# Attention outputs turned by VectorE in 32-squares and divided by their row sums only after the gather

## The chip, the cores and the metric

The kernel runs on one core of one Trainium2 chip. The metric is the device time of the whole program in microseconds (us), as the median of several executions. A core has five engines that run side by side, each through its own list of instructions in order, and that wait for one another by semaphores: TensorE (PE in the profile; PEld is its loading of weights), VectorE (DVE), ScalarE (ACT), GpSimd (POOL) and SyncE (SP, which here only issues transfers). Sixteen DMA engines move data between the chip's main memory (DRAM) and the on-chip memory; matrix products land in a second on-chip memory (PSUM)[...].

## The reference: attention with a threshold, then a layer of experts chosen by hash

```python
def _attn_ref(q, k, v, tau):                       # (8, 8, 576, 64): batch, heads, seq, head_dim
    scale = 1.0 / np.sqrt(q.shape[-1])
    scores = scale * np.matmul(q, k.transpose(0, 1, 3, 2))
    thresh = np.max(scores, axis=-1, keepdims=True) - tau
    scores = np.where(scores >= thresh, scores, -1000000000.0)
    scores = scores - np.max(scores, axis=-1, keepdims=True)
    attn = np.exp(scores)
    attn = attn / (np.sum(attn, axis=-1, keepdims=True) + 1e-09)
    return np.matmul(attn, v)
# the bridge: x[b * 576 + s, 64 * h + d], that is (4608, 512)
def _moe_ref(x, token_ids, w1, w2):                # 8 experts, w1 (8, 512, 1024), w2 (8, 1024, 512)
    expert_idx = token_ids * np.int64(2654435761) % np.int64(8)
    for e in range(8):
        mask = expert_idx == e
        out[mask] = np.maximum(x[mask] @ w1[e], 0.0) @ w2[e]
```

Everything is in 32-bit floats. The division by the row sum can be done before or after the product with v, and also after x has been written to DRAM and gathered again, since one row of x has one sum per head.

## The kernel before

The attention works on 32 pairs of heads (8 batches by 4 pairs; `p` counts pairs, `hp` is the place of the pair among four). A pair has five steps (`s`, or `n` counted over all pairs): step 0 holds the 64 last queries of both heads, steps 1 to 4 hold 128 queries of each head. Per step and head, TensorE makes scores (`score`), VectorE negates them, takes the extreme of each row and moves them out of PSUM (`negate`), ScalarE takes the exponential (`expo`), and VectorE applies the threshold and sums the rows (`mask`). Two steps later TensorE turns the weights (`turn_w`), ScalarE moves them out (`put_wT`), and TensorE multiplies by v (`av_part`), which leaves the output of a pair as 128 rows (head, d) by 576 columns (queries). That output has to be turned, divided and written to the scratch `x_dram`, one row per token:

```python
x_dram = nc.dram_tensor("x_scratch", (N, DIN), FP32, kind="Internal").ap()
x_rows = x_dram.rearrange("n (h d) -> (n h) d", h=HP)
...
def scale_k(p):
    nc.gpsimd.tensor_scalar(out=kts[p][:], in0=kts[p][:], scalar1=keep_any[:],
                            scalar2=SCALE, op0=ALU.mult, op1=ALU.mult)
...
def turn(dst, src, cols):                   # 64x64 transposes on TensorE, two row halves at a time
    for c, (lo, hi) in enumerate(cols):
        for r, c0 in ((0, lo), (1, hi)):
            rows = slice(64 * r, 64 * r + 64)
            nc.tensor.transpose(dst[:, r, 64 * c:64 * c + 64], src[rows, c0:c0 + P],
                                ident[rows, rows])
...
def put_oT(g):                              # PSUM -> SBUF, g = 0: 320 queries, g = 1: 256
    c0, width = ((64, WA), (64 + WA, WB))[g]
    nc.scalar.copy(oT[:, c0:c0 + width], av[:, g, 0:width])

def turn_o():
    turn(av, oT, [(P * (t + 1), P * (t + 1)) for t in range(NQ)] + [(64, 0)])

def add_eps(p):                             # row sums + 1e-9 into rec, on GpSimd
    ...
def put_xm(p):
    rec = recs.pop(p)
    xm = a_x.tile([P, NS, P], FP32, name="xm")
    nc.vector.tensor_tensor(                # PSUM -> SBUF, times 1 / row sum
        out=xm[:].rearrange("p t (j d) -> p t j d", j=2),
        in0=av[:, :, 0:NS * D].rearrange("p j (t d) -> p t j d", t=NS),
        in1=rec[:]. ... .to_broadcast([P, NS, 2, D]), op=ALU.mult)
    r0, c0 = x_place(p)
    nc.sync.dma_start(out=x_dram[r0:r0 + TAIL, c0:c0 + P].rearrange("(t p) m -> p t m", p=P),
                      in_=xm[:, 0:NQ])
    for j in range(2):
        ...                                 # the 64 tail rows, one transfer for each head
```

The order of one step, cut to what touches this:

```python
for n in range(LAST + NS + 1):
    p, s = divmod(n, NS); m = n - 2; q = p - 1
    ...                                     # loads for pair p + 2
    if s == 1 and 0 <= q < NP:
        add_eps(q)
    if s == 1 and p + 1 < NP:
        scale_k(p + 1)
    if s == 2 and 0 <= q < NP:
        nc.vector.reciprocal(recs[q][:], recs[q][:])
    if s == 0 and p >= 2:
        turn_o()
    ...                                     # av_part, negate, expo, put_oT(0) at s == 2, turn_w, put_wT
    if s == 0 and n < LAST:
        next(pieces, None)                  # a piece of the routing; another at s == 3
    if s == 0 and p >= 2 and n != LAST:
        put_xm(p - 2)
    if s == 4 and 0 <= q < NP:
        put_oT(1)
    ...                                     # turn_w, score(n + 1), put_wT
    if 0 < n <= LAST:
        for j in range(heads(n - 1)):
            mask(n - 1, j)
    ...
```

While the last pairs run, three quarters of the rows of expert 0 are gathered already (`fetch_0`), turned by TensorE (`early_xT`) and multiplied (`early_h`, taken in small portions by `fill`); the last quarter follows after the last pair:

```python
for kt in range(KT):
    fetch_0(kt, HP - 1)
fill(FO * 2 * (CO - 1) - 18)
tr = ps_tr.tile([P, 2, 512], FP32, name="tr")
early_xT(tr, 0, KT, CO - 1, CO)
```

The experts 1 to 7 gather their rows by index (`fetch`), VectorE turns them in 32-squares, and transfers put the squares in place:

```python
def turn_x(e):
    for k in range(KT):                     # KT = 5 blocks of 128 rows
        nc.vector.transpose(out=xq[:, :, 32 * k:32 * k + 32],
                            in_=xg_sets[e % 2][k][:].rearrange("p (d a) -> p d a", a=32))
    for g in range(4):
        ...                                 # xq -> xT, 16 transfers
```

Two products with ReLU between them (`gemm1`, `gemm2`, `gemm2_last`) and the scatter of the results end each expert.

Of the kernel before, what the change touches and what calls it, by code (L numbers as in the profile page):

```python
# [20 lines left out]
def kernel(  # L21
# [12 lines left out]
    nc = tc.nc  # L34
# [37 lines left out]
    x_dram = nc.dram_tensor("x_scratch", (N, DIN), FP32, kind="Internal").ap()  # L72
# [16 lines left out]
    keep_any = consts.tile([P, 1], FP32, name="keep_any")  # L89
# [14 lines left out]
    xg_bufs = [consts.tile([P, DIN], FP32, name=f"xg_{i}") for i in range(KT)]  # L104
# [10 lines left out]
    def fetch_0(kt, hp):  # L115
        gather(x_rows, xg_bufs[kt][:, P * hp:P * hp + P], gidx_0[:, kt, hp:hp + 1])
# [11 lines left out]
    with tc.tile_pool(name="a_q", bufs=1) as a_q, \  # L128
# [25 lines left out]
        oT = a_o.tile([P, 64 + S], FP32, name="oT")  # L154
        av = ps_av.tile([P, 2, 512], FP32, name="av")
        kts, rss, recs, scs, nss, stats, ws = {}, {}, {}, {}, {}, {}, {}

        def load_pair(p):
# [23 lines left out]
            for r in range(2):  # L182
                queries(nc.scalar, r, TAIL, S)
            for c0, c1 in ((0, P), (P, TAIL)):
                for r in range(2):
                    queries(nc.sync, r, c0, c1)
# [11 lines left out]
        def scale_k(p):  # L198
            nc.gpsimd.tensor_scalar(out=kts[p][:], in0=kts[p][:], scalar1=keep_any[:],
                                    scalar2=SCALE, op0=ALU.mult, op1=ALU.mult)  # L200
# [4 lines left out]
        def score(n, j):  # L205
# [8 lines left out]
            for h in range(2) if s == 0 else (j,):  # L214
                out_rows = slice(64 * h, 64 * h + 64) if s == 0 else slice(0, P)
                q0, q1 = (TAIL, S) if s == 0 else (P * (s - 1), P * s)
# [94 lines left out]
        def put_oT(g):  # L311
            c0, width = ((64, WA), (64 + WA, WB))[g]
            nc.scalar.copy(oT[:, c0:c0 + width], av[:, g, 0:width])

        def turn_o():
            turn(av, oT, [(P * (t + 1), P * (t + 1)) for t in range(NQ)] + [(64, 0)])

        def x_place(p):
            hp, b = divmod(p, B)
            return b * S, hp * P  # L320

        def add_eps(p):

            rec = a_st.tile([P, 2 * NS], FP32, name="rec")
            rs = rss.pop(p)
            for i, cols in ((0, 9), (9, 1)):
                nc.gpsimd.tensor_scalar(out=rec[:, i:i + cols], in0=rs[:, i - i // 9:i - i // 9 + cols],
                                        scalar1=1e-9, scalar2=None, op0=ALU.add)
            recs[p] = rec

        def put_xm(p):


            rec = recs.pop(p)
            xm = a_x.tile([P, NS, P], FP32, name="xm")
            nc.vector.tensor_tensor(
                out=xm[:].rearrange("p t (j d) -> p t j d", j=2),
                in0=av[:, :, 0:NS * D].rearrange("p j (t d) -> p t j d", t=NS),
                in1=rec[:].rearrange("p (t j) -> p t j", j=2)[:, :, :, None]
                .to_broadcast([P, NS, 2, D]), op=ALU.mult)  # L340
            r0, c0 = x_place(p)
            nc.sync.dma_start(
                out=x_dram[r0:r0 + TAIL, c0:c0 + P].rearrange("(t p) m -> p t m", p=P),
                in_=xm[:, 0:NQ])
            for j in range(2):
                cols = slice(D * j, D * j + D)
                nc.sync.dma_start(out=x_dram[r0 + TAIL:r0 + S, c0 + D * j:c0 + D * j + D],
                                  in_=xm[64 * j:64 * j + 64, NQ, cols])
# [54 lines left out]

# [117 lines left out]
        make_identity(nc, ident[:])  # L521
# [8 lines left out]
        nc.vector.memset(oT[:, 0:64], 0.0)  # L530
        nc.vector.memset(xg_bufs[0][:], 0.0)
        nc.scalar.activation(none_f[:], none_f[:], AF.Exp)
# [16 lines left out]
        def early_xT(tr, k0, k1, c0, c1):  # L549

            blocks = [(kt, co) for kt in range(k0, k1) for co in range(c0, c1)]
            for i, (kt, co) in enumerate(blocks):
                for r in (0, 64):
                    r1 = min(r + 64, TROWS[kt])
                    nc.tensor.transpose(tr[:, r // 64, 64 * i:64 * i + r1 - r],
                                        xg_bufs[kt][r:r1, P * co:P * co + P],
# [62 lines left out]
        with tc.manual_schedule():  # L619

            tr = ps_tr.tile([P, 2, 512], FP32, name="tr")
            for _ in range(16):
# [324 lines left out]
```

## Time and profile before

| | before |
|---|---|
| time, median of 3 | 1008.86 us (1008.33 to 1008.9) |
| span of the profiled execution | 1001.3 us |
| PE busy | 983.8 us (98%) |
| DVE busy | 517.7 us (52%), nearly all of it in the attention |
| ACT busy | 436.9 us (44%) |
| POOL busy | 291.7 us (29%) |
| DMA | 145779 packets, 117.07 MB; 59860 packets under 512 B |
| attention, about | 0 to 454 us of the span |
| passage to the experts, about | 454 to 498 us |
| experts, about | 498 to 1001 us |

The span is one execution under the profiler, a little shorter than the time that is measured around it; differences of the one are read beside differences of the other. A row of groups gives the line of the kernel, the engine, the operation, what it writes and reads, its shape and count, then the total busy time, the mean duration of one in ns, and the idle time of the engine just before, with what ended it. Instructions of one engine overlap at their ends: the next one starts before the last has been completed. So where an engine is full, the cost of an instruction is the distance from its start to the next one's start, which the timeline shows, and not its duration. Busy shares of PE have to be read with care: matmuls are pipelined, and their ends are modelled.

### The profile page before, as it was taken

To read this page: it belongs to the slowest core of one execution; us is meant where nothing else is said; L and a number is where in the kernel's file an instruction comes from. 1 tells how busy PE (TensorE), PEld (TensorE's weight loads), DVE (VectorE), ACT (ScalarE), POOL (GpSimd) and SP (SyncE) were. 2 spreads that over 40 slices of the span, in tenths; PEclk is the share of its full clock that TensorE was granted. 3 is DMA by queue.
4 is the path that set the end of the run, shared out by engine and by line. 5 is a ranking of instruction groups with operands and counts; after the bars stand their busy time and mean duration, and the time that the engine had idled before them with its cause. 6 is when DMAs were issued, how large, how long until landed. Compare 5 with 4: busy or idle time off the path is not lost.

```text
span 1001.3 us, 20487 instructions
## 1 busy us (share of the span) xinstructions
PE 983.8 (98%) x7562; PEld 653.9 (65%) x7562; DVE 517.7 (52%) x1378; ACT 436.9 (44%) x714; POOL 291.7 (29%) x413
## 2 busy tenths in 40 slices
PE   7999999999999999999999999999999999999995
PEld 4666666666666666666766857768578577685773
DVE  7999999999999999994311010010101100200000
ACT  5988888888988889883200000010010000100000
POOL 3233323377676335550321030030210300300101
PEclk9999999999999999999999999999999999999998
DMA  7355544564467677410166344272352533801001
GB/s 182 74 129 141 129 117 112 136 141 107 92 185 169 154 195 194 114 49 25 39 189 185 116 105 143 91 211 89 106 163 84 158 91 104 222 1 39 27 10 57
DMA packets 145779, 117.07 MB, mean 117 GB/s; under 512 B 59860, under 2 KB 120280, under 8 KB 145680
## 3 DMA queue, kind: packets, MB, share of 16 engines
q1 hardware_dynamic: 135408, 96.41, 37.9%
q0 software_dynamic: 7824, 18.91, 6.1%
q8 instruction: 61, 1.00, 0.4%
q10 hardware_dynamic: 2448, 0.44, 0.2%
q14 instruction: 38, 0.31, 0.1%
HBM read 81.99 MB, written 22.37 MB: 104 GB/s over the span
## 4 chain that ended last, share of the span: by engine, by line
PE 87%; issue 6%; SPq 2%; DMA 2%; ACT 1%; DVE 1%; POOL 0%; POOLq 0%; ACTq 0%
PE sc L784 20%; PE av L297 17%; PE sc L219 15%; PE o_ps L802 12%; PE tr L266 10%; PE sc L815 8%; PE sc L579 3%; SPq L835 2%; PE av L266 1%; DMA out_dram<-o_last,gidx 1%; DMA out_dram<-o,gidx 1%; ACT w L244 1%; PE xT_ps L596 0%; PE sc L596 0%; ACT wT_a L287 0%
## 5 line engine op out<-in xcount | busy, mean ns | idle before, releaser
L244 ACT ACTIVATE w<-ns,nmx 128x576 f32<-128x576 f32 x288 | 220.3, 776 | 33.2 <-DVE ns L230 33.1
L784 PE MATMUL sc<-xT,w_sb 128*128 128x304 f32 x896 | 230.4, 419 | 0.0
L255 DVE SCALAR_TENSOR_TENSOR w<-ns,thr,w 128x576 f32<-128x576 f32 x288 | 225.4, 814 | 0.4 <-POOL thr L237 0.4
L784 PEld LDWEIGHTS sc<-xT,w_sb 128*128 128x128 f32 x896 | 170.2, 190 | 61.4 <-issue 3.3
L230 DVE TENSOR_SCALAR_CACHE_REDUCE ns<-sc 128x576 f32<-128x576 f32 x288 | 205.2, 744 | 6.3 <-PE sc L219 5.6
L219 PE MATMUL sc<-k_sb,q 64*128 64x288 f32 (+1 forms) x1280 | 179.2, 426 | 0.6 <-DVE ns L230 0.4
L802 PE MATMUL o_ps<-w_sb,h 128*128 128x512 f32 (+2 forms) x400 | 166.2, 575 | 0.0
L266 PEld LDWEIGHTS tr<-ident,w 64*128 64x128 f32 x2624 | 106.6, 139 | 88.7 <-ACT wT_b L287 26.3
L237 POOL TENSOR_SCALAR thr<-nmx,drop 128x2 f32<-128x2 f32 (+1 forms) x160 | 101.8, 637 | 176.7 <-DVE ns L230 163.4
L792 DVE TENSOR_SCALAR h<-sc 128x608 f32<-128x608 f32 x28 | 22.2, 791 | 240.9 <-PE sc L784 240.9
L266 PE MATMUL tr<-ident,w 64*128 64x64 f32 x2624 | 139.3, 231 | 2.7 <-ACT wT_a L287 2.0
L804 ACT COPY o<-o_ps 128x512 f32<-128x512 f32 (+2 forms) x25 | 14.2, 569 | 274.5 <-PE o_ps L802 248.1
L802 PEld LDWEIGHTS o_ps<-w_sb,h 128*128 128x128 f32 x400 | 74.9, 190 | 86.8 <-issue 84.7
L841 POOL DMA_INDIRECT out_dram<-o,gidx x24 | 23.9, 996 | 324.0 <-ACT o L804 291.4
L219 PEld LDWEIGHTS sc<-k_sb,q 64*128 64x128 f32 (+1 forms) x1280 | 93.0, 179 | 22.9 <-DVE ns L230 9.7
L297 PE MATMUL av<-wT_a,v 128*64 128x320 f32 (+1 forms) x704 | 100.4, 418 | 0.0
L790 ACT ACTIVATE h<-sc 128x608 f32<-128x608 f32 x28 | 19.0, 677 | 182.0 <-PE sc L784 182.0
L815 PE MATMUL sc<-h,w_sb 128*128 128x224 f32 x512 | 98.2, 352 | 0.0
L815 PEld LDWEIGHTS sc<-h,w_sb 128*128 128x128 f32 x512 | 96.9, 190 | 1.1
L287 ACT COPY wT_a<-tr 128x512 f32<-128x512 f32 (+1 forms) x128 | 81.7, 638 | 20.7 <-PE tr L266 20.1
L287 ACT COPY wT_b<-tr 128x512 f32<-128x512 f32 (+1 forms) x128 | 81.2, 634 | 6.4 <-PE tr L266 4.0
L297 PE MATMUL av<-wT_b,v 128*64 128x256 f32 x640 | 83.2, 389 | 0.0
(118 smaller groups left out, 547.9 us busy)
## 6 DMA issues: line engine op xcount, KB each, us to landing
w_sb<-in_moe_w_dram SPq DMA_DIRECT2D x16, 2048.0 KB
q<-in_q_dram SPq DMA_DIRECT2D x62, 288.0 KB
v<-in_v_dram SPq DMA_DIRECT2D x32, 256.0 KB
x_scratch<-xm SPq DMA_DIRECT2D x32, 256.0 KB
xT<-xq SPq DMA_DIRECT2D x84, 80.0 KB
k_sb<-in_k_dram SPq DMA_DIRECT2D x31, 144.0 KB
k_sb<-in_k_dram SPq DMA_DIRECT2D x32, 112.0 KB
o_last<-oq SPq DMA_DIRECT2D x210, 16.0 KB
```

The costliest lines, as they stand in the source:

```text
L219: nc.tensor.matmul(sc[out_rows, i, 0:S2], lhsT=q_sb[rows, h, q0:q1], rhs=k_sb[rows, h], start=True, stop=True)
L230: nc.vector.tensor_scalar(out=ns[:].rearrange("p (i s) -> p i s", i=2), in0=sc[:, :, 0:S2], scalar1=-1.0, scalar2=None, op0=ALU.mult, op1= ...
L237: nc.gpsimd.tensor_scalar(out=thr[:, 0:j + 1], in0=stats[n][0][:, 0:j + 1], scalar1=drop[:], scalar2=None, op0=ALU.add)
L244: nc.scalar.activation(w, nss[n, j][:], AF.Exp, bias=stats[n][0][:, j:j + 1], scale=-1.0)
L255: nc.vector.scalar_tensor_tensor(out=w, in0=nss.pop((n, j))[:], scalar=stats[n][1][:, j:j + 1], in1=w, op0=ALU.is_le, op1=ALU.mult, accum_ ...
L266: nc.tensor.transpose(dst[:, r, 64 * c:64 * c + 64], src[rows, c0:c0 + P], ident[rows, rows])
L287: nc.scalar.copy(dst, tr[:, :, 0:64 * n_c].rearrange("p r (c q) -> p r c q", c=n_c))
L297: nc.tensor.matmul(av[64 * j:64 * j + 64, g, c0:c1], lhsT=v_sb[:, c, 64 * j:64 * j + 64], rhs=wT[g][:, i, c0:c1], start=(c == 0), stop=stop)
L579: nc.tensor.matmul(h_ps[:, i, 0:CH], lhsT=w1_sb[:, co, fo * P:fo * P + P], rhs=xT_0[:, co, i * CH:i * CH + CH], start=(co == 0), stop=(co ...
L784: nc.tensor.matmul(h_ps[:, i, 0:width], lhsT=w1_sb[:, co, fo * P:fo * P + P], rhs=xT[:, co, i * width:i * width + width], start=(co == 0), ...
L802: nc.tensor.matmul(o_ps[:, 0:width], lhsT=h_sb[:, fo, FIRST[kt]:FIRST[kt] + P], rhs=w2_sb[:, fo, cols], start=(fo == 0), stop=(fo == FO - 1))
L815: nc.tensor.matmul(oT_ps[:, i, c * OW:c * OW + OW], lhsT=w2_sb[:, fo, co * P:co * P + P], rhs=h_sb[:, fo, FIRST[KF]:CAP], start=(fo == ord ...
```

## The change

The outputs are no longer turned by TensorE. ScalarE moves each of the two parts of a pair's output out of PSUM as before, and VectorE turns it in squares of 32 by 32, from SBUF to SBUF, one instruction for the part of 320 queries (step 3) and one for the part of 256 (step 0). A turned square has 32 queries as partitions and 32 of the 128 columns of x, so the squares are written by four transfers of 32 partitions, in pieces of 128 bytes. They are not divided: a row of x gets 16 more columns for each pair of heads, in which the row sums (plus 1e-9) are written; a row of a pair is thus 576 bytes where it was 512. Who gathers rows gets the sums with them, and divides: GpSimd for the first three quarters of expert 0, VectorE for the last quarter and for all other experts. This removes TensorE's transposes and VectorE's multiplication and reciprocal from the attention's loop.

So that parts of 32 queries lie at multiples of 32, step 0 of a pair now takes the first 64 queries instead of the last. Three smaller moves come with it: the identity matrix is made ahead of the load of tau, and one more transpose is done as warm-up; the scale of the keys is one operation on tau where it was two; and the clearing of the gather buffers for the experts is GpSimd's work instead of VectorE's. On ScalarE the instructions and their order stay.

```diff
+    DX = P + 16
-    x_dram = nc.dram_tensor("x_scratch", (N, DIN), FP32, kind="Internal").ap()
+    x_dram = nc.dram_tensor("x_scratch", (N, HP * DX), FP32, kind="Internal").ap()
...
+    def normalize(engine, dst, xg, rec):
+        engine.tensor_tensor(
+            out=dst.rearrange("p h (j d) -> p h j d", j=2),
+            in0=xg[:, :, 0:P].rearrange("p h (j d) -> p h j d", j=2),
+            in1=rec[:, :, :, None].to_broadcast([P, rec.shape[1], 2, D]), op=ALU.mult)
...
-        def turn_o():
-            turn(av, oT, [(P * (t + 1), P * (t + 1)) for t in range(NQ)] + [(64, 0)])
+        def turn_o(p, g):
+            if g == 0:
+                xo = a_x.tile([P, S // 32, 32], FP32, name="xo")
+                xos[p] = xo
+            c0, c1 = ((0, WA // 32), (WA // 32, S // 32))[g]
+            nc.vector.transpose(out=xos[p][:, c0:c1],
+                                in_=oT[g][:].rearrange("p (c s) -> p c s", s=32))
...
-        def add_eps(p):
-        ...
-        def put_xm(p):
-        ...
+        def put_x(p):
+            r0, c0 = x_place(p)
+            xo = xos.pop(p)
+            for i in range(4):
+                nc.sync.dma_start(
+                    out=x_dram[r0:r0 + S, c0 + 32 * i:c0 + 32 * i + 32].rearrange(
+                        "(c s) m -> s c m", s=32),
+                    in_=xo[32 * i:32 * i + 32])
+        def put_sums(p):
+            ...                              # sums + 1e-9 into rs on GpSimd, two instructions
+            nc.sync.dma_start(out=x_dram[r0 + 64:r0 + S, c0:c0 + 16].rearrange("(t p) j -> p t j", p=P),
+                              in_=rs[:, 0:4])
+            for j in range(2):
+                width = (1, 15)[j]
+                nc.sync.dma_start(out=x_dram[r0:r0 + 64, c0 + j:c0 + j + width],
+                                  in_=rs[64 * j:64 * j + 64, 4, 0:width])
...
-        make_identity(nc, ident[:])          # now first thing in the ordered part, ahead of tau's load
...
-            for _ in range(16):
+            for _ in range(17):
                 nc.tensor.transpose(tr[:, 0, 0:P], ident[:], ident[:])
...
-            nc.vector.tensor_scalar(out=keep_any[:], in0=tau_in[:], scalar1=0.0, ...)
+            nc.vector.tensor_scalar(out=k_scale[:], in0=tau_in[:], scalar1=0.0, scalar2=SCALE,
+                                    op0=ALU.is_ge, op1=ALU.mult)
...
                 if s == 1 and 0 <= q < NP:
-                    add_eps(q)
+                    put_sums(q)
-                if s == 2 and 0 <= q < NP:
-                    nc.vector.reciprocal(recs[q][:], recs[q][:])
-                if s == 0 and p >= 2:
-                    turn_o()
...
+                if s == 3 and 0 <= q < NP:
+                    turn_o(q, 0)
                 if s == 0 and p >= 2 and n != LAST:
-                    put_xm(p - 2)
+                    turn_o(p - 2, 1)
+                    put_x(p - 2)
...
+                if s == 1 and 0 <= k < KT:   # k = p - (NP - KT)
+                    nc.gpsimd.tensor_copy(xr_0[0][:, k], xg_bufs[k][:, 0:HP - 1, P:P + 2])
+                if n == LAST - 3:
+                    nc.vector.reciprocal(xr_0[0][:], xr_0[0][:])
+                for k in {LAST - 2: (0, 1), LAST - 1: (2, 3, 4)}.get(n, ()):
+                    normalize(nc.gpsimd, xg_bufs[k][:, 0:HP - 1, 0:P], xg_bufs[k][:, 0:HP - 1],
+                              xr_0[0][:, k])
...
-            fill(FO * 2 * (CO - 1) - 18)
+            fill(FO * 2 * (CO - 1) - 26)
+            for kt in range(KT):
+                nc.vector.reciprocal(xr_0[1][:, kt], xg_bufs[kt][:, HP - 1:HP, P:P + 2])
+                normalize(nc.vector, xg_bufs[kt][:, HP - 1:HP, 0:P], xg_bufs[kt][:, HP - 1:HP],
+                          xr_0[1][:, kt])
+            fill(8)
...
+        def normalized(k, xg):
+            xr, xn = xr_bufs[k % 2], xn_bufs[k % 2]
+            nc.vector.reciprocal(xr[:], xg[:, :, P:P + 2])
+            normalize(nc.vector, xn[:], xg, xr)
+            return xn[:].rearrange("p h d -> p (h d)")
...
         def turn_x(e):
             for k in range(KT):
                 nc.vector.transpose(out=xq[:, :, 32 * k:32 * k + 32],
-                                    in_=xg_sets[e % 2][k][:].rearrange("p (d a) -> p d a", a=32))
+                                    in_=normalized(k, xg_sets[e % 2][k]).rearrange(
+                                        "p (d a) -> p d a", a=32))
...
-        for xg in xg_sets[1]:
-            nc.vector.memset(xg[:], 0.0)
+            for xg in xg_sets[1]:
+                nc.gpsimd.memset(xg[:], 0.0)
+                nc.gpsimd.memset(xg[:, :, P:DX], 1.0)
```

## The prediction, written before the changed kernel had run

> **What bounds the kernel now.** I read the chain of work that ended last first, for the engine that sets the end, then windows of one pair each, then the timeline of one pair row by row, and at last the groups by form for durations.
>
> ```profile
> PE 87%; issue 6%; SPq 2%; DMA 2%; ACT 1%; DVE 1%; POOL 0%; POOLq 0%; ACTq 0%
> ```
>
> TensorE carries the chain. But a chain prefers the engine that is never idle, so I asked for single pairs of the attention (columns: us, then busy time of PE, PEld, DVE, ACT, POOL with instruction counts, granted clock, DMA share, GB/s):
>
> ```profile
> 160.00:173.90 13.90, 13.90 (x176) 8.80 (x174) 13.64 (x42) 12.19 (x21) 4.22 (x8) 1.00 0.52 128
> 299.50:313.40 13.90, 13.90 (x177) 8.80 (x174) 13.83 (x39) 12.28 (x22) 9.48 (x12) 1.00 0.55 139
> 340.00:353.90 13.90, 13.90 (x178) 8.80 (x174) 13.78 (x40) 12.27 (x21) 4.41 (x8) 1.00 0.75 168
> ```
>
> Two engines are full in a pair: PE 13.90 of 13.90 us and DVE 13.64 to 13.83. ScalarE has 1.6 us to spare. Which of the two full ones sets the pace shows in their starts. TensorE in the timeline (start, duration, then what):
>
> ```profile
> 300.27 0.71 PE L219 MATMUL sc<-k_sb,q 64*64 64x288 f32 x8
> 300.91 0.53 PE L266 MATMUL av<-ident,oT 64*128 64x64 f32 x10
> 301.27 0.41 PE L266 MATMUL tr<-ident,w 64*128 64x64 f32 x8
> 301.52 1.19 PE L219 MATMUL sc<-k_sb,q 64*128 64x288 f32 x8
> ...
> 304.71 0.46 PE L266 MATMUL tr<-ident,w 64*128 64x64 f32 x8
> 305.01 0.70 PE L219 MATMUL sc<-k_sb,q 64*128 64x288 f32 x4
> ```
>
> One block starts where the one before has issued its last product; the single starts within a block lie 0.06 us apart for two 64-column transposes, 0.24 for 288 columns, 0.26 for 320. I find no hole in a quiet pair: TensorE's work alone is 13.90 us. VectorE (and the GpSimd row beside it):
>
> ```profile
> 301.73 0.82 DVE L336 TENSOR_TENSOR xm<-av,rec 128x640 f32<-128x640 f32 x1
> 302.47 0.81 DVE L255 SCALAR_TENSOR_TENSOR w<-ns,thr,w 128x576 f32<-128x576 f32 x1
> ...
> 304.62 0.75 DVE L230 TENSOR_SCALAR_CACHE_REDUCE ns<-sc 128x576 f32<-128x576 f32 x1
> 304.89 0.75 POOL L199 TENSOR_SCALAR k_sb<-k_sb,keep_any 128x576 f32<-128x576 f32 x1
> 305.30 0.94 DVE L255 SCALAR_TENSOR_TENSOR w<-ns,thr,w 128x576 f32<-128x576 f32 x1
> 306.17 0.21 DVE L670 RECIPROCAL rec<-rec 128x10 f32<-128x10 f32 x1
> 306.30 0.69 DVE L230 TENSOR_SCALAR_CACHE_REDUCE ns<-sc 128x576 f32<-128x576 f32 x1
> ```
>
> From start to start, a mask (L255) takes 0.74 us, a negation (L230) 0.675, the division of the outputs (L336) 0.74, the reciprocal 0.13. One mask in a pair takes 0.87, the one that runs beside GpSimd's scaling of keys. So a quiet pair costs VectorE 9 x 0.74 + 9 x 0.675 + 0.74 + 0.13 + 0.13 = 13.74 us. The small operations of the routing, two slots a pair until pair 27, add 5.6 us of starts in all, 0.2 a pair: 13.9. The two engines are in balance within 0.1 us. From the first turn of outputs (34.76 us) to the 31st (453.68) 30 pairs pass in 418.9 us, 13.96 each.
>
> In the experts TensorE is full and VectorE idle (40.3 of 380 us busy between 600 and 980), so what the change adds there has room.
>
> [...] In the packet records, 128 bytes take 13 ns (median, on-chip moves), 256 bytes 18, 512 bytes 29: small packets cost more a byte, but the size alone is not a cliff. 128-byte pieces to DRAM are not in this trace.
>
> **The change part by part.**
>
> *TensorE, removed.* The ten transposes of outputs. Scores, turned outputs and turned weights take 301.52 - 300.91 = 0.61 us up to the next scores; without the outputs, a block of 8 behind another kind takes 305.01 - 304.71 = 0.30. Saved: 0.31 a pair, so 13.59 us. The idle 0.44 us that the weight loads show ahead of L266 is no further gain: the scores still issue then.
>
> *VectorE, removed and added.* Off: 0.74 + 0.13 = 0.87. On: two turns from SBUF. The sizes for that:
>
> ```profile
> L336 DVE TENSOR_TENSOR xm<-av,rec 128x640 f32<-128x640 f32 x32 | 26.1, 817 | 0.1
> L856 DVE STREAM_TRANSPOSE xq<-xh 128x512 f32<-128x512 f32 x20 | 14.1, 709 | 45.9 <-issue 36.2 <-DMA xh<-x_scratch,gidx_x 9.5
> ```
>
> Four such turns in a row (526.63 us) take 2.52: (2.52 - 0.71) / 3 = 0.60 from start to start. The division takes 0.74 for 640 columns. Both fit 1.04 ns a column and 0.07 us besides, so 320 columns cost 0.40, 256 cost 0.33, together 0.73. Net 0.14 less: 13.60 in a quiet pair, 13.79 with the routing.
>
> *The pair after.* TensorE 13.59, VectorE 13.6 to 13.8, ScalarE unchanged at 12.3. VectorE takes the pace over, which cuts the gain from 0.31 to about half. With a loss of 0.03 to 0.05 where two balanced engines wait for each other (the pair before lost 0.06), I choose 13.82 for the 27 pairs with routing and 13.65 for five without: 27 x 0.14 + 5 x 0.25 = 5 us gained.
>
> *Passage to the experts.* TensorE drops two more turns with their waits, 453.34 to 453.99 and 470.51 to 470.96: 1.1 us. Against that, five divisions of 384 columns stand on GpSimd in front of the turning of expert 0. One key scaling of 576 columns takes 0.75[...]. Two run behind the thresholds of the step before last, three behind the last at about 453.6, so blocks 2 and 3 are ready near 454.6 and 455.6 where TensorE wants them at 453.7: up to 1.9 us of waiting, part of it before waits that are there anyway. I book 1.3. Net +0.2.
>
> The last quarter of expert 0 hangs on this:
>
> ```profile
> 475.72 1.10 POOL L110 DMA_INDIRECT xg<-x_scratch,gidx  x1 [18.49 <-DMA x_scratch<-xm]
> ...
> 481.06 0.99 POOL L110 DMA_INDIRECT xg<-x_scratch,gidx  x1 [0.30 <-issue]
> ...
> 487.53 0.58 PEld L555 LDWEIGHTS tr<-ident,xg 64*128 64x128 f32 x10 [0.41 <-issue]
> ```
>
> The last gather, issued at 481.06 with 3.6 us to land, is there at 484.7; TensorE comes at 487.5, 2.8 us later. The outputs now leave about 1.5 us earlier (no TensorE turn), in four transfers instead of three (0.6 us more), and the last division adds 0.4. Hidden.
>
> *Transfers.* A pair writes 2304 pieces of 128 bytes and 640 of up to 64, for 640 pieces before. With 13 to 18 ns and 9 ns on 16 engines: 2.2 to 3 us, less 1.1 for what goes, so 1 to 2 us of 13.9: the share of 0.52 to 0.75 rises by about 0.1. Loads run two pairs ahead. SyncE issues 7 transfers more per pair minus 3, 2.4 us; it idled 152.9 us for TensorE in front of L174, over 5 a pair. Hidden.
>
> *Experts.* Per expert five reciprocals and five multiplications, about 5 x 0.73 = 3.7 us more of VectorE ahead of the turns. For expert 1 the placing transfers end near 516 us, its product starts at 531. Hidden. *Start.* The earlier identity may gain 0.3 us. *Sum.* -5 + 0.2 - 0.3 = -5: 1003.5 us.
>
> **The rivals.** *TensorE alone sets the pace*, and VectorE's waits fold away: 32 x 0.31 and the passage, 998 us. For it: quiet pairs are exactly 13.90. Against: VectorE's own sum. *The wait moves to VectorE for good*: turns in the middle of a step delay the second negation and so ScalarE and the next turn of weights; a pair stays at 13.9 and GpSimd's divisions cost 2 us: 1010. *The small writes choke DRAM*: if a 128-byte write cost several times 18 ns, the share would near 1 where the 2 MB weight loads run (already 0.75), and loads come late: 1015 to 1040. Nothing in the 256-byte writes of the tail (18 ns) points there.
>
> **Range and chances.** Between the first two rivals lies 998 to 1010; the middle weighs most, so 8 in 10 for 998 to 1009. Faster by 2% would need 20 us, twice what TensorE sheds: 0.02. Slower by 2% needs the third rival: 0.04. Same: 0.94.
>
> **What would show it.** Right: pairs 13.6 to 13.85 apart, DVE busy near the whole pair while PE shows waits for VectorE or ScalarE; turns of 320 and 256 columns about 0.40 and 0.33 from start to start; a wait of TensorE on GpSimd of 1 to 2 us near 450; experts as long as before, 65.5 us each. Wrong: pairs at 13.6 and PE without holes (first rival), pairs at 13.9 (second), waits of TensorE for loads, or packets of 128 bytes far above 18 ns (third), or a gap of TensorE near 485.

## The result, and the profile after

The changed kernel takes 1024.22 us (median of 4, 1021.16 to 1026.75) beside 1008.88 us for the kernel before, measured with it: ratio 1.015, 95% interval 1.012 to 1.018. It is slower by 1.5%, where 0.5% faster was predicted.

The chain of work that ended last, its first line. TensorE had 87% of it before; now VectorE and "issue" have a tenth each or nearly:

```profile
PE 68%; issue 10%; DVE 8%; ACT 4%; DMA 3%; SPq 3%; POOL 2%; POOLq 0%; DVEq 0%; ACTq 0%
```

Windows of one pair, as before (us, then busy time of PE, PEld, DVE, ACT, POOL with instruction counts, granted clock, DMA share, GB/s), a quiet one first. Then a stretch late in the attention (PE alone):

```profile
160.00:173.90 13.90, 13.61 (x166) 8.61 (x164) 13.70 (x42) 12.44 (x21) 4.95 (x8) 1.00 0.74 132
```

```profile
388.00:394.00 6.00, 0.86 (x16) 0.99 0.86 113
394.00:401.00 7.00, 5.75 (x38) 0.52 1.06 331
```

The quiet pair is what the prediction drew: PE down from 13.90 to 13.61 us, DVE full. The late stretch is not in the prediction at all: TensorE works 0.86 us of 6, and then runs at half its clock (granted clock 0.52). Nor does the share of the DMA engines rise by 0.1 in the quiet pair: it goes from 0.52 to 0.74.

The groups by form that matter (busy, mean ns of one, idle time before them), first two of before:

```profile
L199 POOL TENSOR_SCALAR k_sb<-k_sb,keep_any 128x576 f32<-128x576 f32 x31 | 23.1, 746 | 5.7 <-DMA k_sb<-in_k_dram 2.9
L255 DVE SCALAR_TENSOR_TENSOR w<-ns,thr,w 128x576 f32<-128x576 f32 x288 | 225.4, 814 | 0.4 <-POOL thr L237 0.4
```

```profile
L333 DVE STREAM_TRANSPOSE xo<-oT 128x320 f32<-128x320 f32 x32 | 16.2, 505 | 0.0
L333 DVE STREAM_TRANSPOSE xo<-oT 128x256 f32<-128x256 f32 x32 | 14.0, 438 | 0.0
L211 POOL TENSOR_SCALAR k_sb<-k_sb,k_scale 128x576 f32<-128x576 f32 x31 | 55.2, 1781 | 6.7 <-DMA k_sb<-in_k_dram 3.9
L267 DVE SCALAR_TENSOR_TENSOR w<-ns,thr,w 128x576 f32<-128x576 f32 x288 | 225.4, 815 | 16.1 <-POOL thr L249 15.9
L124 POOL TENSOR_TENSOR xg<-xg,xr 128x384 f32<-128x384 f32 x5 | 6.0, 1221 | 0.0
```

Two things stand out. The scaling of the keys on GpSimd, a line that the prediction passed over, went from 0.75 us to 1.78. And VectorE's masks now wait 15.9 us for the thresholds that GpSimd makes (0.4 before). What held GpSimd up is in the timeline (start, duration, what, and in brackets the idle time before it and what ended it):

```profile
385.84 2.19 SPq L344 DMA_DIRECT2D x_scratch<-xo  x4
...
388.13 0.47 SPq L360 DMA_DIRECT2D x_scratch<-rs  x1
...
388.69 1.11 SPq L364 DMA_DIRECT2D x_scratch<-rs  x2
...
392.79 1.09 POOL L114 DMA_INDIRECT xg<-x_scratch,gidx  x1 [10.65 <-issue]
...
394.28 0.82 DVE L267 SCALAR_TENSOR_TENSOR w<-ns,thr,w 128x576 f32<-128x576 f32 x1 [6.77 <-POOL thr L249]
...
395.25 0.69 PE L278 MATMUL tr<-ident,w 64*128 64x64 f32 x8 [6.39 <-DVE w L267]
```

Read upwards. TensorE waits 6.39 us for a mask, the mask 6.77 for a threshold, the threshold stands on GpSimd behind the first early gather of expert 0, and that gather has waited 10.65 us, for nothing that the profile names ("issue"). It reads rows anywhere in the scratch, so it comes after every write to the scratch ahead of it in the program, also those of the quarter that it does not read (in E4, with that quarter in a tensor of its own, no early gather waits over 1.0 us). The newest of them left SyncE from 385.84 to 389.8, though their turned outputs had been ready at 376.3 (VectorE's turn began at 375.81) and their sums at 378.3. In the kernel before (its second trace, E5) the writes are out by 377.9, and the gather waits 0.85 us:

```profile
376.17 0.54 SPq L342 DMA_DIRECT2D x_scratch<-xm  x1
376.75 1.14 SPq L347 DMA_DIRECT2D x_scratch<-xm  x2
...
381.07 1.14 POOL L110 DMA_INDIRECT xg<-x_scratch,gidx  x1 [0.85 <-issue]
```

The idle time of SyncE for TensorE that the prediction leaned on is gone ahead of this gather. Waits of SyncE from 335 to 385 us (total, times, longest), first E5, then after:

```profile
SPq L174 <- PE sc L219: 12.0, 3, 5.8
SPq L196 <- DMA w_sb<-in_moe_w_dram: 2.1, 1, 2.1
```

```profile
SPq L208 <- DMA w_sb<-in_moe_w_dram: 6.7, 2, 3.5
...
SPq L186 <- PE sc L231: 0.5, 1, 0.5
```

Where the time went, in stretches. A pair is taken from ScalarE's copy of its first turned weights (L282 before, L294 after) to that of the next; the passage ends at the first product with the second weights of expert 0. Pairs count from 1, p in the code from 0. The first trace of the kernel before is of a quick execution (1003.3 us beside the usual 1008.9), so differences are taken from its second trace (E5, span 1005.6), except for E9 to E12, whose kernel before took 1003.4 us and which the text sets beside the first. All in us.

| stretch | before (E5) | after | E1 | E2 | E3 | E4 | E7 | E13 | E16 |
|---|---|---|---|---|---|---|---|---|---|
| to the first copy | 12.29 | -1.1 | -1.2 | -0.3 | -0.8 | -1.2 | -0.7 | +0.2 | +0.1 |
| pair 1 | 15.43 | +3.9 | +0.9 | +2.6 | +2.7 | +1.1 | +2.4 | +0.7 | +1.7 |
| pairs 2 to 13 | 168.59 | -1.3 | -1.3 | 0.0 | -1.3 | -1.3 | -1.3 | +0.2 | -1.3 |
| pairs 14 to 25 | 169.91 | +0.8 | -1.2 | -0.1 | +1.0 | -1.9 | -1.9 | +3.0 | -1.0 |
| pairs 26 to 31 | 85.69 | +11.5 | +12.9 | -0.1 | -1.2 | -1.7 | +7.9 | +6.7 | +0.4 |
| passage | 63.33 | +2.6 | +2.7 | 0.0 | +1.0 | +2.6 | +2.7 | 0.0 | -1.1 |
| experts | 479.01 | 0.0 | 0.0 | 0.0 | +1.9 | +0.8 | 0.0 | 0.0 | 0.0 |
| after the last product | 11.34 | +0.1 | +0.2 | -0.1 | +3.2 | +3.3 | +0.1 | +0.2 | 0.0 |

So 11.5 of the 16.4 us between the two traces lie in pairs 26 to 31, 2.8 at the start and 2.6 in the passage. Pair 27 alone is 8.4 us longer (22.78 for 14.34): the wait of 6.39 us, and 6.8 us at half clock from 393.9 on.

### The profile page after: what moved, and what is told of

Read it like the earlier page. It is cut to its first block, busy times and chain, and to the rows that moved or that the text cites. A ratio compares the mean times of both kernels' runs of the same rounds, so it can differ in the third digit from the quotient of the medians.

```text
span 1022.0 us, 20106 instructions
## 1 busy us (share of the span) xinstructions
PE 983.9 (96%) x7243; PEld 651.1 (64%) x7243; DVE 546.4 (53%) x1454; ACT 440.0 (43%) x714; POOL 318.8 (31%) x434
## 4 chain that ended last, share of the span: by engine, by line
PE 68%; issue 10%; DVE 8%; ACT 4%; DMA 3%; SPq 3%; POOL 2%; POOLq 0%; DVEq 0%; ACTq 0%
PE sc L817 19%; PE o_ps L835 12%; PE av L309 10%; PE sc L231 8%; PE sc L848 8%; PE tr L278 7%; DVE w L267 4%; DVE ns L242 3%; PE sc L596 3%; ACT wT_a L299 2%; SPq L868 2%; ACT w L256 1%; DMA x_scratch<-rs 1%; DMA k_sb<-in_k_dram 1%; DMA out_dram<-o_last,gidx 1%
## 5 line engine op out<-in xcount | busy, mean ns | idle before, releaser
L267 DVE SCALAR_TENSOR_TENSOR w<-ns,thr,w 128x576 f32<-128x576 f32 x288 | 225.4, 815 | 16.1 <-POOL thr L249 15.9
L242 DVE TENSOR_SCALAR_CACHE_REDUCE ns<-sc 128x576 f32<-128x576 f32 x288 | 208.3, 748 | 9.6 <-PE sc L231 7.3
L278 PEld LDWEIGHTS tr<-ident,w 64*128 64x128 f32 x2624 | 110.6, 140 | 121.2 <-ACT wT_a L299 42.0
L231 PE MATMUL sc<-k_sb,q 64*128 64x288 f32 (+1 forms) x1280 | 182.5, 430 | 2.2 <-DVE ns L242 1.6
L278 PE MATMUL tr<-ident,w 64*128 64x64 f32 x2624 | 141.4, 233 | 21.0 <-DVE w L267 12.3
L249 POOL TENSOR_SCALAR thr<-nmx,drop 128x2 f32<-128x2 f32 (+1 forms) x160 | 87.6, 548 | 164.6 <-DVE ns L242 152.9
L309 PE MATMUL av<-wT_a,v 128*64 128x320 f32 (+1 forms) x704 | 103.0, 426 | 0.0
```

The lines of the kernel that those rows point to most:

```text
L231: nc.tensor.matmul(sc[out_rows, i, 0:S2], lhsT=q_sb[rows, h, q0:q1], rhs=k_sb[rows, h], start=True, stop=True)
L242: nc.vector.tensor_scalar(out=ns[:].rearrange("p (i s) -> p i s", i=2), in0=sc[:, :, 0:S2], scalar1=-1.0, scalar2=None, op0=ALU.mult, op1= ...
L249: nc.gpsimd.tensor_scalar(out=thr[:, 0:j + 1], in0=stats[n][0][:, 0:j + 1], scalar1=drop[:], scalar2=None, op0=ALU.add)
L267: nc.vector.scalar_tensor_tensor(out=w, in0=nss.pop((n, j))[:], scalar=stats[n][1][:, j:j + 1], in1=w, op0=ALU.is_le, op1=ALU.mult, accum_ ...
L309: nc.tensor.matmul(av[64 * j:64 * j + 64, g, c0:c1], lhsT=v_sb[:, c, 64 * j:64 * j + 64], rhs=wT[g][:, i, c0:c1], start=(c == 0), stop=stop)
```

## The experiments

Theory A: the scaling of the keys in its new form is slow on GpSimd. Theory B: SyncE issues too many transfers, its writes to the scratch come late, and the early gathers wait for them in front of the thresholds. Rival C: the 128-byte packets crowd the DRAM. Theory D: the divisions on GpSimd hold the passage. Each kernel was timed beside the kernel before (1008.0, 1008.2, 1003.4 and 1008.2 us in the groups E1 to E4, E5 to E8, E9 to E12 and E13 to E16), so the ratio is what compares; why the third group is quicker is not known.

| run | what | us | ratio, 95% interval |
|---|---|---|---|
| E1 | after, keys scaled in two operations | 1019.21 | 1.0108 (1.0092 to 1.0123) |
| E2 | before, keys scaled in one operation | 1009.31 | 1.0009 (1.0002 to 1.0015) |
| E3 | after, two scratches | 1014.66 | 1.0067 (1.0052 to 1.0082) |
| E4 | E1 and E3 | 1009.89 | 1.0019 (1.0012 to 1.0025) |
| E5 | before again | 1008.48 | 1.0002 (0.9994 to 1.0010) |
| E6 | E1, writes ahead of loads | 1016.68 | 1.0080 (1.0066 to 1.0094) |
| E7 | E1, packets of 2304 bytes | 1014.95 | 1.0059 (1.0046 to 1.0072) |
| E8 | E6, divisions spread | 1016.92 | 1.0075 (1.0061 to 1.0089) |
| E9 | E7, one transfer in place of four | 1004.35 | 1.0008 (1.0000 to 1.0016) |
| E10 | E4, divisions spread | 1004.76 | 1.0011 (1.0005 to 1.0018) |
| E11 | E1, divisions spread, gathers and weight loads later | 1005.97 | 1.0025 (1.0015 to 1.0035) |
| E12 | E11, writes ahead of loads | 1003.81 | 1.0002 (0.9994 to 1.0011) |
| E13 | before, 15 transfers a pair | 1016.55 | 1.0079 (1.0066 to 1.0092) |
| E14 | E1, 14 transfers a pair | 1014.82 | 1.0064 (1.0045 to 1.0082) |
| E15 | E12, weights of expert 1 in the passage | 1006.32 | 0.9973 (0.9962 to 0.9984) |
| E16 | E15 and the joined tail of E14 | 1005.48 | 0.9967 (0.9955 to 0.9979) |

**E1 and E2: the form of the scaling.**

```diff
 # E1, in scale_k
-  in0=kts[p][:], scalar1=k_scale[:], scalar2=None, op0=ALU.mult
+  in0=kts[p][:], scalar1=k_scale[:], scalar2=1.0, op0=ALU.mult, op1=ALU.mult
 # E2, the kernel before
-  scalar1=keep_any[:], scalar2=SCALE, op0=ALU.mult, op1=ALU.mult
+  scalar1=k_scale[:], scalar2=None, op0=ALU.mult
```

> The changed kernel with the scaling of the keys on GpSimd back in a form of two operations (times k_scale, times 1.0), nothing else touched. Theory A (the form with one operation is slow on GpSimd and holds up the thresholds behind it): the scaling falls from 1.73 to about 0.75 us, the wait of VectorE for thr from 15.9 us to under 8, the start is 2 to 3 us shorter and pairs 15 to 24 lose their 3.5 us; in all 5 to 7 us off 1024, so 1017 to 1019. Theory B (SyncE's queue of transfers and the early gathers that wait for the newest writes on GpSimd): the ten or more us of pairs 26 to 31 stay. Rival C (small packets crowd the DRAM): time unchanged within 1 us.

> The kernel before with nothing changed but the scaling of the keys in the form with one operation (times k_scale). Theory A: the scaling rises from 0.75 to about 1.7 us, a mask beside it on VectorE is stretched longer, and the kernel is 2 to 6 us slower than the kernel before, 1011 to 1015. If the 1.73 us came from the DMA traffic of the changed kernel and not from the form: scaling 0.75 and time 1009.

The groups, first of E1, then of E2:

```profile
L211 POOL TENSOR_SCALAR k_sb<-k_sb,k_scale 128x576 f32<-128x576 f32 x31 | 24.0, 775 | 6.8 <-DMA k_sb<-in_k_dram 3.9
```

```profile
L199 POOL TENSOR_SCALAR k_sb<-k_sb,k_scale 128x576 f32<-128x576 f32 x31 | 53.9, 1738 | 5.9 <-DMA k_sb<-in_k_dram 3.0
```

The microsecond is the form, and nothing else: an operation more makes the scaling 1 us shorter, in either kernel. E1 comes from 1.5% down to 1.08%, 4.3 us; in its trace pairs 14 to 25, where scatters fill GpSimd, are 2.0 us shorter, and the start 3.1. The start holds a second difference, though: TensorE ran there at half clock for 10.2 us in the changed kernel and in E2, and for 3.4 in E1 and E5 (more in the next part), so not all of the 3.1 belongs to the form, nor of the 2.3 us that E2's start is longer. In the time E2 loses 0.09% (0.02 to 0.15), 0.9 us where 2 to 6 were expected: elsewhere a microsecond more on GpSimd is hidden. Theory A holds for under a third of the loss; VectorE's wait for thresholds is still 13.1 us in E1 where under 8 was expected, so the rest is something else.

**E3 and E4: gathers that need not wait.**

```diff
-x_dram = nc.dram_tensor("x_scratch", (N, HP * DX), FP32)
+x_lo = nc.dram_tensor("x_scratch", (N, (HP - 1) * DX), FP32)
+x_hi = nc.dram_tensor("x_last", (N, DX), FP32)   # quarter 3; experts gather from both
```

> The changed kernel with the scratch for the outputs in two DRAM tensors, quarters 0 to 2 in one and quarter 3 in the other, so that the early gathers of quarters 0 to 2 no longer wait for the writes of the pairs that are just done; the experts gather from both (five gathers more each). Scaling of keys still in one operation. Theory B: the waits of 10.65 and 5.50 us ahead of the gathers go, pairs 26 to 31 lose 9 to 13 us, in all 1011 to 1015. Rival C: pairs 26 to 31 stay within 3 us, about 1022.

> Both mends at once: two scratches and the scaling in two operations. Theories A and B together: 1024 less 5 to 7 less 9 to 13, so 1004 to 1010, at or below the kernel before; pairs then about 0.1 us shorter than before throughout. Rival C: not under 1018.

In E3 pairs 26 to 31 go from +11.5 to -1.2, in E4 to -1.7. E4's waits between 370 and 450 us (total, times, longest):

```profile
POOL xg L116 <- issue: 2.4, 14, 0.3
...
POOL xg L116 <- DMA x_scratch<-xo: 1.0, 1, 1.0
...
PE tr L287 <- ACT wT_a L308: 0.8, 4, 0.2
...
PE tr L287 <- issue: 0.4, 2, 0.2
```

No gather waits over 1.0 us, and TensorE's matrix products 0.2 at most. Yet all small packets are still written: in pairs 26 to 28 the DMA engines are busier (share 0.93, for 0.82 in E1 and 0.67 in E5), so a busy DRAM alone (rival C) does not make the loss. A and B add up: of the 1.5%, 0.42 and 0.83 apart, 1.31 together. E4 is still 0.2% above the kernel before, though its attention is 4.9 us shorter: the passage has +2.6, and the cure costs 4.1 of its own (0.8 in the experts and 3.3 after the last product, where 35 gathers more have been issued; why the end grows was not tried).

**E5: the kernel before again.**

> The kernel before, unchanged, for a second trace of it: the first trace's span (1001.3 us) lies 7.6 us under its measured time, those of the other kernels 1.7 to 2.5 us under theirs. If the first trace is a quick execution: span here 1005 to 1007, with the start or the pairs 14 to 31 longer than in the first trace. If not: 1001 again. Time 1008.

Span 1005.59, 4.3 more than in its first trace, 2.7 of it in pairs 14 to 25 and 2.1 in 26 to 31: so far apart lie two traces of one kernel there, while pairs 2 to 13 agree within 0.1.

**E6: the order on SyncE.**

```diff
-  if s == 0: load_pair(p + 2); load_v(p + 1)
+  if s == 2: load_pair(p + 2); load_v(p + 1)   # behind put_x (s = 0) and put_sums (s = 1)
```

> The changed kernel with the scaling in two operations and the loads of the next pairs put behind the writes of outputs and sums on SyncE (loads at the third step of a pair in place of the first); still one scratch, so the early gathers still wait for the newest writes. Theory B (SyncE comes late with these writes because up to eight loads stand ahead of them): the waits ahead of the early gathers fall from up to 10.65 us to under 3 us, 9 to 13 us off the 1019 of the two-operation form: 1006 to 1010. If the wait comes from the writes themselves (landing late, small packets): 1016 or more. If loads then come late, waits of TensorE or GpSimd for keys appear and it is above 1020.

Only 0.28% (2.8 us), not 9 to 13 us. SyncE in E6, the writes of one pair earlier than the first gather, and that gather:

```profile
363.50 0.58 SPq L131 DMA_DIRECT2D w_sb<-in_moe_w_dram  x1
364.17 5.45 SPq L344 DMA_DIRECT2D x_scratch<-xo  x4
369.72 2.20 SPq L360 DMA_DIRECT2D x_scratch<-rs  x1
372.02 1.65 SPq L364 DMA_DIRECT2D x_scratch<-rs  x2
...
386.75 1.13 POOL L114 DMA_INDIRECT xg<-x_scratch,gidx  x1 [7.23 <-DMA k_sb<-in_k_dram]
```

Ahead of the loads or behind them, the seven writes stand in one queue with a 2 MB load, and here they are what comes behind it: 9.5 us for seven issues, one of which alone lasts 3.7. The gather waits 7.23 us where under 3 was expected. The order moves the shortage, it does not end it.

**E7, E9 and E13: size of packets or number of issues.** E7 and E9 leave the layout of x out and write the outputs in pieces of 2304 bytes; E7 keeps four transfers a pair, E9 makes one of them. E13 does the reverse to the kernel before: same bytes and packets, seven writes in place of three.

```diff
 # E7: 4 of these; E9: one, with 128 rows
-  out=x_dram[r0:r0 + S, c0 + 32 * i:c0 + 32 * i + 32]  as "(c s) m -> s c m"
+  out=bass.AP(tensor=x_dram.tensor, offset=(p * P + 32 * i) * S, ap=[[S, 32], [1, S]])
 # E13, put_xm of the kernel before
-  1 write of xm[:, 0:4], 2 of the rest
+  4 writes of xm[:, t], 3 of the rest (64 rows of one head in two halves)
```

> The changed kernel with the scaling in two operations, and the outputs written as 32 pieces of 2304 bytes a transfer to a wrong place in the scratch, so the layout is left out: same number of transfers and same order on SyncE, but 128 packets a pair in place of 2304 (and 12 small fill transfers in place of 9). Theory B (issues and order): 1017 to 1020, as with small packets, and the gathers wait as long. Rival C (small packets crowd the DRAM or make the issue itself slow): waits ahead of the gathers under half, 1008 to 1013.

> As the kernel with packets of 2304 bytes (layout left out, scaling in two operations), but the outputs of a pair go out as one transfer of 128 partitions in place of four of 32: 12 transfers a pair on SyncE in place of 15, bytes and packets the same. Theory B1 (it is the number of issues on SyncE, 0.5 to 0.65 us each, in the stretch with the 16 reads of the slot tables and the weight loads): 2 us of SyncE a pair less, the gather of pair 26 leaves 4 us or more earlier, pairs 26 to 31 lose most of the 10 us that they still cost: 1005 to 1010. If the count does not matter and the wait is in the landing of the writes of sums or in the weight loads: 1013 to 1016.

> The kernel before, its three writes of the outputs cut into seven (the block of 512 rows by its four row tiles, one of the two rests in halves): 15 transfers a pair on SyncE as in the changed kernel, bytes and packet sizes as before, no other change. If the number of issues is the cause (theory B1): the early gathers of pairs 26 and 27 wait long, pairs 26 to 31 get 8 to 12 us longer, ratio to the kernel before 1.007 to 1.012. If the count alone does not do it (the small packets or the place of the writes of sums are needed): within 0.2%.

E7 is below what B alone expected and above what C alone expected: with the packets 18 times as long, 0.49% go, 4.9 us, and the first gather waits 7.9 us for 11.5 in E1. With three issues fewer as well, E9, another 0.51% goes, 5.1 us, and E9 is level with the kernel before that was measured with it (E7 and E9 lie in different groups, so this step is less sure). E13 is the plainest: the kernel before loses 8.3 us for nothing but four more issues a pair, 3.0 of it in pairs 14 to 25 and 6.7 in 26 to 31. Its timeline at the first gather:

```profile
383.51 1.97 SPq L343 DMA_DIRECT2D x_scratch<-xm  x4
...
385.55 2.32 SPq L346 DMA_DIRECT2D x_scratch<-xm  x3
...
390.00 1.14 POOL L110 DMA_INDIRECT xg<-x_scratch,gidx  x1 [5.76 <-DVE ns L230]
...
391.54 0.82 DVE L255 SCALAR_TENSOR_TENSOR w<-ns,thr,w 128x576 f32<-128x576 f32 x1 [2.23 <-POOL thr L237]
...
392.51 0.47 PE L266 MATMUL tr<-ident,w 64*128 64x64 f32 x8 [1.36 <-DVE w L255]
```

It is the chain of the changed kernel, link by link, in the old one. (The wait of 5.76 is put down to VectorE, which had long been done.) The gather left 2.1 us after the last write was issued (385.55 + 2.32), in the changed kernel 3.0 us after (388.69 + 1.11).

How both parts come together shows in the time for which issues hold SyncE between 320 and 450 us, added up from the trace:

| | E5 | E9 | E13 | E7 | E1 |
|---|---|---|---|---|---|
| transfers | 107 | 113 | 146 | 138 | 137 |
| of them over 1 us | 8 | 6 | 7 | 7 | 12 |
| us of SyncE in all | 65.2 | 64.8 | 80.0 | 78.9 | 84.6 |
| pairs 26 to 31 | 0 | +0.7 (from the first trace) | +6.7 | +7.9 | +12.9 |

The count gives 14 to 15 us of the 19. The small packets give the other 5 to 6: a write of outputs lasts 0.51 us in the median in E1, hardly other than in E7 (0.42) or E5 (0.54), but more issues are held for over 1 us. Held time alone is no loss: E4 holds SyncE for 91.8 us and E16 for 81.3, and their pairs 26 to 31 are at -1.7 and +0.4, for there the gathers hardly wait.

**E14: one issue fewer.** The two writes of the tail's sums become one, with the sums at columns 0 and 8; its pieces are of 32 bytes where they were of 4 and 60.

```diff
-  for j in range(2): x_dram[r0:r0 + 64, c0 + j:...] <- rs[64 * j:64 * j + 64, 4, 0:(1, 15)[j]]
+  one write, ap=[[8, 2], [W, 64], [1, 8]] <- rs[:, 4, 0:8]
```

> The changed kernel with two operations and the two writes of the tail's sums joined into one transfer of 128 pieces of 32 bytes (sums at columns 0 and 8 in place of 0 and 1): 14 transfers a pair in place of 15, output complete. Theory B1, a third of what three transfers fewer brought (0.51%): ratio from 1.0108 to about 1.009. If only a threshold counts: unchanged, or all of it.

It brings 0.44%, nearly what three issues did, and pairs 26 to 31 come from +12.9 to +4.8 in its trace (a trace 2.7 us quicker than the median). The cost is not linear in the issues. One reason stands in the traces: half clock followed the longer waits, 13.7 us of it in pairs 26 to 31 in E1, 3.4 in E14 and none in E4 and E16, where TensorE waited 0.4 us at most.

**E8, E10, E11, E12: divisions, gathers, weight loads.**

```diff
 # E8, E10, E11, E12: spread over the pairs
-  all five GpSimd divisions at n = LAST - 2 and LAST - 1
+  block k in step 4 of pair 27 + k, its reciprocals in step 3   # p of the code
 # E11, E12
-  one gather each in steps 2, 3, 4; weights of expert 1 loaded at p = 24, 26
+  one gather in step 3, two in step 4; weights at p = 28, 30
```

> As the one before last (two operations, writes ahead of loads), and the five divisions of expert 0 on GpSimd spread over pairs 27 to 31, one a pair, in place of all five in the last two steps. Theory D (divisions of 1.2 to 1.3 us at the passage hold TensorE for 2 us): 1.5 to 2.5 us less than the kernel with the divisions in the last steps, TensorE's waits for GpSimd in front of the turns of expert 0 gone. If the masks beside the divisions cost as much in the pairs as the passage gains: no difference.

> Two operations, two scratches, and the five divisions of expert 0 spread over pairs 27 to 31. With two scratches nothing of GpSimd waits for the newest writes, so the pairs stay as in the kernel with two scratches (1009.9), and the passage loses the 2 to 3.5 us that it lost beside the one scratch (from the first of the last steps to the second product of expert 0, 53.8 us before the spreading, 50.1 after it there; 51.2 in the kernel before): 1006 to 1008, at the kernel before or just below. If the divisions in the pairs cost masks as much: 1009 to 1010.

> One scratch; two operations; divisions spread; the 2 MB weight loads of expert 1 moved from pairs 24 and 26 to pairs 28 and 30; and the three early gathers of a pair moved from its steps 2, 3, 4 to one in step 3 and two in step 4, farthest behind the writes that they wait for. Theory B: the wait at pair 26 falls from over 10 us to under 4 us, and 8 us or more go: 1005 to 1010. If the writes are still late at pair 26 because of the slot-table reads alone: 1010 to 1014.

> The kernel before this one with the writes of outputs and sums ahead of the loads on SyncE as well (loads at the third step of a pair). Theory B: the gathers wait under 2 us, 1003 to 1008, below the kernel before. If the writes, which wait for the gathers of the pair before them to land, now hold the loads back: waits for keys and over 1010.

In all four the passage goes to -1.1 us, 3.8 below that of the divisions at the end. In E8 pairs 26 to 31 take it back (13.9 above E5, for 9.9 in E6). With the gathers freed, E10, little of it stays either: 1.0011 for 1.0019 in E4, under 1 us of the 3.7, as in the case that was expected if the divisions cost masks in the pairs; its pairs 26 to 31 are 1.1 us longer than in the first trace of before, where E4's were 1.7 shorter than in E5. E11 stays 0.25% above the kernel before (first gather: a wait of 4.6 us) and E12 is level with it (0.4 us, but 4.7 at p = 29), each a little over what was expected: with the loads of 2 MB moved to p = 28 and 30 the pair p = 29 is 4.1 us longer than in the first trace of before in E11 and 2.4 in E12. In E12 its writes waited 5.7 us for the gathers of p = 28 to land, issued together with the load.

**E15 and E16: the mends together.**

```diff
-  weights of expert 1 at p = 28, 30
+  after the last pair, steps 2 and 3   # E16: with E14's joined tail
```

> The best so far (two operations, divisions spread, gathers in steps 3 and 4, writes ahead of loads), with the 2 MB weights of expert 1 loaded only after the last attention pair in place of pairs 28 and 30, where the writes of pair 30 still waited about 5 us behind them. Theory B: pairs 30 and 31 lose 2 to 3 us, ratio 0.997 to 0.999, below the kernel before. If the loads then delay the last gathers or expert 1: over 1.000.

> All mends on one scratch: the one just named and the joined tail as well, 14 transfers a pair. Ratio 0.996 to 0.998: what the prediction gave for the change itself (0.9948) without the start, where the changed kernel still shows about 1 us more.

Both ratios come out as expected. E16 has the lowest ratio, 0.33% (0.21 to 0.45) below the kernel before, not to be told from E15 (0.27%). Its waits from 370 to 450 us:

```profile
POOL xg L114 <- issue: 2.4, 9, 0.6
...
PE tr L278 <- ACT wT_a L299: 1.6, 5, 0.4
...
POOL xg L114 <- DVE xo L333: 1.2, 4, 0.3
```

## Why the prediction was wrong, step by step

**The pair: mechanism right, gain a little smaller.** "Saved: 0.31 a pair, so 13.59 us" is 13.61 in the window. The two turns, sized at 0.40 and 0.33 from start to start, take 0.43 (383.51 to the next start at 383.94) and 0.37 (375.81 to 376.18), so VectorE sheds 0.07 in place of 0.14; quiet pairs are 0.11 shorter (1.3 / 12), where 0.14 to 0.25 was predicted. VectorE takes the pace over, as written. With A and B taken away (E4) the three stretches of pairs give -1.3 - 1.9 - 1.7 = -4.9 us, but that it meets the 5 predicted is partly luck: E5 is itself 4.8 us longer in pairs 14 to 31 than the first trace of before, and 31 pairs of 0.11 are 3.4. The gain is there; it was overlaid.

**"SyncE ... it idled 152.9 us for TensorE in front of L174, over 5 a pair. Hidden": the step that failed.** Its arithmetic was an average over the attention. ("7 transfers more per pair minus 3, 2.4 us" is right: 15 for 11.) From 340 us on SyncE also reads the slot tables (16 issues, 8.7 us in E1), and from p = 20 to 26 it sends four loads of 2 MB and waits behind them. From 335 to 385 us E5 has 12.0 us of idle time for TensorE, over 3 a pair; the 2.4 would still have fitted, but with them the waits behind the loads of 2 MB grow too (2.1 to 6.7 us), and 0.5 us is left: the queue is full, and the writes leave some 10 us after their data are ready. And the prediction asked only whether loads come late. The reader that could not wait was another: the gathers, whose wait for all writes was in its own quotation for the last quarter ("[18.49 <-DMA x_scratch<-xm]") and was not carried over to the fifteen early ones. E13 shows that four issues suffice for 8.3 us, E3 and E4 that the gathers' wait is the way by which it reaches TensorE.

**The scaling of the keys: left out.** The diff turned it from two operations to one, and the prediction took it as it was ("from this row ... 0.75"). It is 1.78 us, and 4.3 us of the loss (E1): 2.0 of it among the scatters in the traces (2.9 from E3 to E4), some at the start.

**"The small writes choke DRAM": partly.** Against the reason given ("128 bytes far above 18 ns") the 128-byte packets of the attention took 13 ns in the median and 15.0 in the mean, as the prediction sized them, and the rival was given 0.04 for that. Yet packets of 2304 bytes take 4.9 us off (E7), while E4 keeps the small ones and loses nothing in the pairs. So they add to the loss where a gather waits for the writes, and do not make it. What part of that is a later landing and what a held issue was not separated.

**Passage: mechanism right, size wrong.** "I book 1.3. Net +0.2": the waits on GpSimd are where they were put, at blocks 2 and 3 of expert 0 (counted from 0):

```profile
473.11 0.40 PE L572 MATMUL sc<-ident,xg 64*128 64x64 f32 x6 [1.15 <-POOL xg L124]
474.41 0.40 PE L572 MATMUL sc<-ident,xg 64*128 64x64 f32 x6 [0.90 <-POOL xg L124]
```

That is 2.05 us, for a division of 384 columns takes 1.22 us (3.91 / 3 = 1.30 in the row of three) where the 1.0 that lies between the booked 454.6 and 455.6 was the author's estimate, which no operation in the trace of before shows. VectorE's of 512 take 0.70, so here GpSimd took 2.3 times as long a column (3.18 ns for 1.36). The gain of 1.1 from the two dropped turns is exact: -1.1 with the divisions spread. The missing 1.6 us are the clock. In the trace of the changed kernel the stretches of half clock begin whole multiples of 3.413 us apart (at 15.03, 393.91, 414.39 and 475.83 us, the last three 111, 117 and 135 such steps behind the first), so it can be divided into such windows, and E14's was divided likewise. In the changed kernel both waits fall into one window, and the next is at half clock; in E14, with the same two waits, a border lies between them, no half clock follows, and the passage is +1.0 = 2.1 - 1.1 (windows of after, then of E14: us, PE busy, granted clock, DMA share, GB/s):

```profile
472.42:475.83 3.41, 1.82 (x26) 1.00 0.57 85
475.83:479.24 3.41, 3.41 (x12) 0.50 0.13 12
```

```profile
459.43:462.85 3.42, 2.27 (x42) 1.00 0.02 5
462.85:466.26 3.41, 2.51 (x31) 1.00 0.58 87
466.26:469.67 3.41, 3.41 (x23) 1.00 0.12 11
```

**Last quarter, experts: right.** No gap where the last quarter is turned; the experts are equal to 0.0 us. **Start: wrong**, -0.3 against +2.8: 1.1 us are gained up to the first copy and 3.9 lost in pair 1. Across the traces the start (from E5) follows the number of such windows at half clock in pair 1 (3.4, 6.8 or 10.2 us). With one (E1, E4, E5 and the first trace of before) it is -0.3 to +0.5, with two (E3, E6, E8, E9, E11 to E16) +0.6 to +1.9, with three (after, E2, E7, E10) +1.7 to +2.8. With three, the slow scaling makes 0.6 to 1.1 of it (after and E2 beside E7 and E10). Why it is one, two or three was not tried.

## What to carry to other kernels

A queue's idle time is read in the stretch that matters, not as a mean: count its issues a pair there, with bursts and long loads, before four more are called hidden. Ask of every writer that is moved or multiplied which reader waits for it in order, and what stands behind that reader on its engine. And a line of the diff that only seems tidier, one operation for two, is costed like any other. A wait of TensorE can cost more than its length, for the clock behind it: here 2.05 us of waits in the passage brought 1.6 us more at half clock.

## What the runs showed of the hardware that was not expected

On GpSimd a tensor times one scalar, 128x576 in fp32, took 1.74 to 1.79 us, and times two scalars 0.75 to 0.78 (both kernels, E1 to E4). Whether other operations differ so was not tried.

In the trace of the changed kernel an issue of a transfer held SyncE 0.37 us in the median for a load of 2 MB (0.58 at most), 0.47 and 0.59 for the two kinds of writes of sums, 0.51 for a write of outputs and 0.65 for keys, so the transfer with the most bytes held it shortest. Of the four writes of outputs behind a load of 2 MB in E6 one held it for 3.7 us.

TensorE's clock fell to half for 10.24 us at 15.03 in the changed kernel, for 6.83 at 393.91 and for 3.41 at 414.39 and at 475.83: once, twice or three times 3.413 us. Behind the two waits in the passage (1.15 and 0.90 us in the changed kernel and in E14) the granted clock over the next 5 us was 0.66 in the changed kernel and in E1 and 0.69 in E4, but 1.00 in E14, where a border of the windows lies between the waits, and in E3. From 370 to 476 us the changed kernel has these windows at full clock with over 1 us of idle time: behind those from 390.50, 410.98 and 472.42 us, with TensorE busy for 0.00, 1.50 and 1.82 of 3.41 us, came half clock; behind those from 387.08 and 441.70, busy for 1.78 and 2.19, came full clock. Here a window less than half idle was enough for the fall. 1.78 and 1.82 stand in the wrong order, but TensorE's busy time is modelled, so where the border lies was not shown. The slow start lasted 10.2 us (the changed kernel, E2, E10), 6.8 (E16) or 3.4 (E1, E4, E5); why it differs was not shown.
